# Keys with queries, and decays, loaded with 128 rows, and a new order of all queues planned for loads of 385 GB/s

## The chip, the cores and the metric

One core of a Trainium2 chip runs the kernel. Its engines work side by side, each through its own list of instructions in order: PE (TensorE, the matmuls; its weight loads are listed as PEld), DVE (VectorE), ACT (ScalarE), POOL (GpSimd), and SP (SyncE), which here only issues DMAs. An instruction that waits for another engine or for a DMA holds up everything behind it on its own engine. The metric is the device time of one execution in microseconds (us), lower being better. The kernel before took 775.98 us in the median of three runs (774.26 to 776.66).

## The reference

```python
for t in range(S):                                    # S = 768, per batch (4) and head (8), head_dim D = 48
    state = alpha[:, :, t, :, None] * state + np.einsum('bhd,bhe->bhde', k[:, :, t], v[:, :, t])
    y[:, :, t] = np.einsum('bhd,bhde->bhe', q[:, :, t], state)
x = y.transpose(0, 2, 1, 3).reshape(4 * 768, 384)     # 3072 tokens
h = x @ w_in;  x = (h * np.cos(h)) @ w_out            # first MLP, 384 -> 2048 -> 384
h = np.maximum(np.maximum(x @ w1, x @ w2), x @ w3)    # second MLP, 384 -> 768 -> 384
out = h @ w_out2
```

A linear attention with a decay per key dimension feeds two dense layers in a row. All inputs are float32.

## The kernel before, in words

The 3072 tokens are cut into six units of 512. In each unit attention goes by four pairs of heads; a pair's keys and queries, and its decays, lie with one head in partitions 0 to 47 and the other in 64 to 111, so that 112 rows are used. Per pair three loads come in on SP's queue: decays `al` (112 x 522 float32), keys with queries `kq` (112 x 1024) and values `v` (128 x 384). The recurrence is done in chunks. DVE forms running products of the decays by scans, POOL multiplies the keys by one of them and the queries by the other, PE transposes keys and multiplies, DVE masks the products with a triangle, PE multiplies the masked products by the values. Unit 0, where no state comes in, is done by `att0` with chunks of 128; units 1 to 5 are done by `turn` and `visit` with chunks of 64, slipped between the matmuls of the first MLP of the unit before.

The dense layers run in three passes of a rounded format: each float32 factor is split into a high part and a low part, and high x high, low x high and high x low are added. In the first MLP a step (`moe1`, 96 of them, 16 a unit) takes nine matmuls of 128x128 by 128x512 into one PSUM bank (lines L658 to L660), then cos on ACT and DVE (L666 to L684), then nine matmuls into three accumulators (L689 to L691). The second MLP (L740 to L765) takes unit after unit when all six have passed the first.

The weights of the first MLP, 32 blocks of 384 KB, two for each of 16 steps (`wi` and `wo`), come as raw 8-byte words into four buffers `raw`. Each block is converted when it has landed: ACT makes a top half (L360), DVE joins words (L361), ACT rounds to the high part (L365), and the low part is a subtraction. For the `wi` blocks that is POOL's (L369, into `wil`). For the `wo` blocks, `LOD = (1, 3)` makes it DVE's (L367, into `wol`), and the joined words then stand in a PSUM bank.

The order of all work is set in advance. `build` records every operation with its engine, an estimated duration, what it reads and writes, and a due time. `Program.order` then plays the program through with these estimates, each engine taking among its ready operations the one with the smallest due time, and the sequence it arrives at is written out as the program. The constants at the head of the file (`FIRST`, `ATT0`, `ATTS`, `W1E`, `EARLY`, `V2` and so on) set due times; `LANDED` and a rate for DMAs set when a load is taken to have landed. Where the plan has PE idle for long enough early on, it puts matmuls that nobody reads (L909).

Places to find in the code below: `att0` with the loads at L411 to L413, the scans at L418 and L424, POOL's products at L420 and L426, the masks at L458, values by masked products at L473, and the split of a result into high (ACT, L489) and low part. For pair `k < XLE` the low part is made by PE and ACT (L491, L492), else by DVE (L494). `prepare` with the loads at L509 to L511, the scans L514 and L518, and POOL's products L517 and L520; `visit` with its matmuls at L556, L560, L574 and L581.

Of the kernel before, what the change touches and what calls it, by code (L numbers as in the profile page):

```python
# [62 lines left out]

XLE = 1
MKP = 0
GATE, GSTEP = 1, 1
LOD = (1, 3)

W1E = 12
MOE_EARLY = 4  # L70
EARLY = 3
FIRST = -4
ATT0 = -1
ATTS = 3.3
VIS, VEND, VQ = 4.0, 13, 0.2
LARGE, STALL, PATIENT = 2, 0.6, 1.5
V2, V2S, TA = 16.0, 3.2, 1.0
NA = (NU - 1) * NP
# [5 lines left out]
class Program:  # L84
# [9 lines left out]
    def __init__(self):  # L94
        self.ops = []
        self.last_write = {}
        self.readers = {}
        self.of_bank = {}

    def op(self, eng, dur, fn, reads=(), writes=(), due=0.0, nbytes=None, port=False, tiled=False, count=6):  # L100
        n = len(self.ops)
        deps = set()
        for k in reads:
            if k in self.last_write:
                deps.add(self.last_write[k])
# [12 lines left out]
        deps.discard(n)
        port = port or (eng == "Pool" and nbytes is None)
        self.ops.append((eng, dur, nbytes, fn, sorted(deps), due, port, tiled, count))  # L120
        return n

    def order(self, banks, limit):
# [50 lines left out]
        for _ in range(n):  # L174
# [32 lines left out]
            if nbytes is not None:  # L207
                dma_free = max(dma_free, end + (0.65 if e == "SP" else 1.05)) + nbytes / 295e3
                end = dma_free + LANDED
# [65 lines left out]

HW, LANDED, SLACK = 0.46, 1.6, 0.0


@with_exitstack
def tile_kernel(ctx, tc, aa, qk, vv, wt, outT):  # L280
# [32 lines left out]

    kq_b = [ap.tile([PR, 2 * HB], F32, name=f"kq{i}") for i in range(NKQ)]
    v_b = [ap.tile([P, N2, 2, D], F32, name=f"v{i}") for i in range(NV)]
# [74 lines left out]
    def att0(k, p, t0):  # L390
        na, nk, nv, n2 = k % NIN, k % NKQ, k % NV, k % 2
        t, kq_, v, s = al_b[na], kq_b[nk], v_b[nv], s_b[p]
        vk, kk_ = ("v", nv), nk
        gf, kg = g_b[k % NGS], ("g", k % NGS)
        if k == 2:
            v, vk = q_b[2][:, 0:2 * N2 * D].rearrange("p (i j e) -> p i j e", i=N2, j=2), ("q", 2)
        if k == 3:
            v, vk = v_b[2], ("v", 2)
            t, na = inv_b[0], "iv0"
            gf, kg = inv_b[1][:, 0:AL], ("iv1",)  # L400
            kq_, kk_ = yy_b[1].bitcast(F32).rearrange("p a b -> p (a b)")[0:PR], "yy1"
        g = gf[:, 0:AP].rearrange("p (c t) -> p c t", c=N2)
# [97 lines left out]
    def prepare(n, t0):  # L500
# [271 lines left out]
    def build():  # L772
# [210 lines left out]
```

## Time and profile before

| | |
|---|---|
| runs of before, us | 774.26, 776.66, 775.98 |
| profiled execution, us | 773.87 |
| its span, us | 772.1 |
| PE busy | 762.5 us, 99% |
| DVE busy | 429.4 us, 56% |
| ACT busy | 348.4 us, 45% |
| POOL busy | 125.3 us, 16% |
| granted clock of TensorE | 1.0 throughout |

The span is from the first to the last instruction on the core; the profiled execution's own time is 1.8 us more. A share over the whole span says little here, since the first 90 us, with attention of two units and the weights' conversion, are full on every engine, and the rest is matmuls almost alone. PE's busy share counts matmuls that wait in the array for each other: a matmul of 512 columns is listed with some 390 ns, while in a dense stretch one starts every 0.23 us. So PE's loss is read from the starts of its instructions.

### The profile page before, as it was taken

How to read it: one execution, taken by the hardware profiler on the slowest of the kernel's cores; microseconds unless marked ns; L12 is line 12 of the kernel's file. 1: busy time of each engine (PE TensorE's matmuls, PEld its weight loads, DVE VectorE, ACT ScalarE, POOL GpSimd, SP SyncE). 2: the span in 40 equal slices, each digit the busy share in tenths (PEclk: the TensorE clock that was granted, in tenths of full speed). 3: DMA queues.
4: the chain of work that ended last, by engine and by line, in shares of the span. 5: the costliest groups of instructions: out<-in, count | busy, mean ns of one | idle time of the engine just before them, and what ended most of it. 6: DMA issues, size and time to landing. Idle time of an engine off the chain costs nothing.

```text
span 772.1 us, 14185 instructions
## 1 busy us (share of the span) xinstructions
PE 762.5 (99%) x5863; PEld 626.0 (81%) x5863; DVE 429.4 (56%) x720; ACT 348.4 (45%) x669; POOL 125.3 (16%) x133
## 2 busy tenths in 40 slices
PE   8899999999999999999999999999999999999998
PEld 6687788888888888888888888888888888888886
DVE  8799998686856776765557754432221312213121
ACT  5688756455555655465568754411121211111121
POOL 5555432120301121110023301100000000000000
PEclk9999999999999999999999999999999999999999
DMA  9977633232311231121027504220020200200001
GB/s 287 277 236 217 190 106 102 54 97 75 110 53 55 86 110 43 42 90 36 8 82 269 168 20 138 88 81 28 14 96 28 82 27 14 96 24 4 22 20 42
DMA packets 26464, 69.84 MB, mean 90 GB/s; under 512 B 3392, under 2 KB 6464, under 8 KB 26400
## 3 DMA queue, kind: packets, MB, share of 16 engines
q1 hardware_dynamic: 26400, 68.93, 28.3%
q8 instruction: 46, 0.75, 0.4%
q14 instruction: 18, 0.15, 0.1%
HBM read 52.80 MB, written 14.16 MB: 87 GB/s over the span
## 4 chain that ended last, share of the span: by engine, by line
PE 88%; DVE 1%; ACT 1%; issue 0%; DVEq 0%; ACTq 0%
PE ps L740 10%; PE ps L742 10%; PE ps L741 9%; PE acc L689 8%; PE acc L691 8%; PE ps L658 8%; PE acc L690 8%; PE ps L659 7%; PE ps L660 7%; PE ps L765 3%; PE ps L763 3%; PE ps L764 3%; PE ps L556 1%; PE ps L574 1%; PE ps L581 1%; PE ps L530 1%
## 5 line engine op out<-in xcount | busy, mean ns | idle before, releaser
L658 PE MATMUL ps<-xt,wih 128*128 128x512 f32 x288 | 115.1, 400 | 0.6 <-ACT woh L365 0.6
L689 PE MATMUL acc<-gh,woh 128*128 128x512 f32 x288 | 114.0, 396 | 0.1
L691 PE MATMUL acc<-gl,woh 128*128 128x512 f32 x288 | 112.4, 390 | 0.4 <-DVE gl L684 0.4
L659 PE MATMUL ps<-xt,wih 128*128 128x512 f32 x288 | 112.4, 390 | 0.2 <-DVE xt L494 0.2
L660 PE MATMUL ps<-xt,wil 128*128 128x512 f32 x288 | 112.3, 390 | 0.0
L690 PE MATMUL acc<-gh,wol 128*128 128x512 f32 x288 | 112.2, 390 | 0.0
L667 DVE SCALAR_TENSOR_TENSOR q<-q,ps 128x512 f32<-128x512 int32 x96 | 65.4, 682 | 49.8 <-ACT q L666 49.5
L750 DVE TENSOR_TENSOR ps<-t,ps 128x512 f32<-128x512 f32 x36 | 25.1, 696 | 106.7 <-PE ps L742 106.7
L666 ACT ACTIVATE q<-ps 128x512 int32<-128x512 f32 x96 | 57.1, 595 | 59.6 <-PE ps L660 58.0
L668 ACT ACTIVATE q<-q 128x512 f32<-128x512 f32 x96 | 60.5, 631 | 42.0 <-DVE q L667 41.3
L672 DVE TENSOR_TENSOR gl<-q,gh 128x512 fp32r<-128x512 f32 x80 | 57.8, 724 | 32.9 <-ACT gh L671 30.5
L751 ACT ACTIVATE h<-ps 128x512 fp32r<-128x512 f32 x36 | 21.6, 600 | 113.4 <-DVE ps L750 113.4
L670 DVE TENSOR_TENSOR q<-q,ps 128x512 f32<-128x512 f32 x80 | 54.7, 684 | 27.5 <-ACT q L668 26.5
L671 ACT ACTIVATE gh<-q 128x512 fp32r<-128x512 f32 x80 | 50.2, 629 | 35.1 <-DVE q L670 32.1
L748 DVE TENSOR_TENSOR t<-t,ps 128x512 f32<-128x512 f32 x36 | 24.8, 688 | 71.3 <-PE ps L742 71.2
L691 PEld LDWEIGHTS acc<-gl,woh 128*128 128x128 f32 x288 | 54.1, 188 | 12.7 <-DVE gl L684 1.3
L658 PEld LDWEIGHTS ps<-xt,wih 128*128 128x128 f32 x288 | 54.1, 188 | 12.5 <-ACT woh L365 1.0
L689 PEld LDWEIGHTS acc<-gh,woh 128*128 128x128 f32 x288 | 54.0, 188 | 12.2 <-ACT gh L679 0.5
L660 PEld LDWEIGHTS ps<-xt,wil 128*128 128x128 f32 x288 | 54.1, 188 | 11.7 <-POOL wil L369 0.5
L659 PEld LDWEIGHTS ps<-xt,wih 128*128 128x128 f32 x288 | 54.1, 188 | 11.4 <-DVE xt L494 0.9
L690 PEld LDWEIGHTS acc<-gh,wol 128*128 128x128 f32 x288 | 54.1, 188 | 10.5
L768 ACT ACTIVATE y<-ps 128x512 f32<-128x512 f32 x18 | 10.8, 600 | 93.2 <-PE ps L765 93.2
(147 smaller groups left out, 1449.1 us busy)
## 6 DMA issues: line engine op xcount, KB each, us to landing
raw<-in_wt SPq DMA_DIRECT2D x56, 384.0 KB, 3.8
kq<-in_qk SPq DMA_DIRECT2D x23, 448.0 KB, 4.3
x1d<-yy SPq DMA_DIRECT2D x18, 512.0 KB, 2.7
xt<-x1d SPq DMA_DIRECT2D x18, 512.0 KB, 5.0
al<-in_aa SPq DMA_DIRECT2D x23, 228.4 KB, 2.7
outT<-y SPq DMA_DIRECT2D x18, 256.0 KB, 2.0
v<-in_vv SPq DMA_DIRECT2D x23, 192.0 KB, 4.6
xt<-yy SPq DMA_DIRECT2D x30, 64.0 KB, 3.1
```

Source lines behind the costliest of these rows:

```text
L658: pe.matmul(ps, wi["h"][:, f, cc], xt[:, cc, 0], start=(cc == 0), stop=False)
L659: pe.matmul(ps, wi["h"][:, f, cc], xt[:, cc, 1], start=False, stop=False)
L660: pe.matmul(ps, wi["l"][:, f, cc], xt[:, cc, 0], start=False, stop=(cc == NR - 1))
L667: op("DVE", dve(HB), lambda: ve.scalar_tensor_tensor(q, q.bitcast(I32), -TWOPI, ps, ALU.mult, ALU.add), [hk], [qk], m)
L668: op("Act", act(HB), lambda: se.activation(q, q, AF.Sin, bias=0.5 * math.pi), (), [qk], m)
L672: op("DVE", dve(HB), lambda: ve.tensor_tensor(gl, q, gh.bitcast(F32), ALU.subtract), [qk, ("gh", gn)], [("gl", gn)], m, port=True)
L689: pe.matmul(acc[c], oh, gh, start=(f == 0), stop=False)
L690: pe.matmul(acc[c], ol, gh, start=False, stop=False)
L691: pe.matmul(acc[c], oh, gl, start=False, stop=(f == NF1 - 1))
L740: pe.matmul(ps, w2t["h"][m][:, f, cc], xt[:, cc, 0], start=(cc == 0), stop=False)
L741: pe.matmul(ps, w2t["h"][m][:, f, cc], xt[:, cc, 1], start=False, stop=False)
L742: pe.matmul(ps, w2t["l"][m][:, f, cc], xt[:, cc, 0], start=False, stop=(cc == NR - 1))
```

## The change

Five edits are made in one.

1. `kq` and `al` get 128 rows instead of 112, on the host as in SBUF; the loads move all 128. Views of the first 112 rows do the arithmetic as before, so no other instruction changes its shape.
2. `XLE` goes from 1 to 3: for pairs 1 and 2 of unit 0 also, the low part is made by one matmul and an ACT copy instead of a DVE subtraction.
3. `LOD = (1,)`: every second `wo` block now stays in SBUF, and its low part is POOL's (8 blocks of 32).
4. In `att0` the masked products go through three buffers in turn (two `a` and the second `q`) instead of two.
5. The planner takes 385 GB/s for loads instead of 295 and 1.0 us until landing instead of 1.6; its constants are other ones, and single events are shifted in their due times by a table. The new rule with `HOLD` is empty and never applies.

```diff
-XLE = 1
+XLE = 3
...
-LOD = (1, 3)
-
-W1E = 12
...
+LOD = (1,)
+
+W1E = 7
...
+HOLD, HOLD_END = {}, 32.0
...
+        if eng != "PE" or not self.fixed:
+            due += self.shift[nbytes is not None]
...
-                dma_free = max(dma_free, end + (0.65 if e == "SP" else 1.05)) + nbytes / 295e3
+                dma_free = max(dma_free, end + (0.65 if e == "SP" else 1.05)) + nbytes / RATE
...
-HW, LANDED, SLACK = 0.46, 1.6, 0.0
+RATE = 385e3
+HW, LANDED, SLACK = 0.46, 1.0, 0.0
...
-    kq_b = [ap.tile([PR, 2 * HB], F32, name=f"kq{i}") for i in range(NKQ)]
+    kq_f = [ap.tile([P, 2 * HB], F32, name=f"kq{i}") for i in range(NKQ)]
+    kq_b = [t[0:PR] for t in kq_f]
...
-        op("SP", HW, lambda: nc.sync.dma_start(kq_, qk[0, p]), (), [kk, kq], first - 3.9, dma(PR * 2 * HB * 4))
+        op("SP", HW, lambda: nc.sync.dma_start(kq_to, qk[0, p]), (), [kk, kq], first - 3.9, dma(P * 2 * HB * 4))
...
-        aks = [[("a", j, 0), ("a", j, 1)] for j in range(2)]
+        slots = [(a_b[j].rearrange("p a b c -> p (a b) c").rearrange("p a c -> p (a c)"), [("a", j, 0), ("a", j, 1)]) for j in range(2)] + [(q_b[1], [("q", 1)])]
+        slots = [slots[(2 * k + j) % 3] for j in range(2)]
...
-        for _, _, f, a in sorted(events):
+        for n, (_, _, f, a) in enumerate(sorted(events)):
+            G.shift, G.fixed = SHIFT.get(n, (0.0, 0.0)), f is moe1
             f(*a)
+        G.shift, G.fixed = (0.0, 0.0), True
...
-    aa = _np.ascontiguousarray(aa.reshape(NU, NP, 2 * UP, ALW)[:, :, :PR])
-    qk = _np.ascontiguousarray(qk.reshape(NU, NP, 2 * UP, 2 * HB)[:, :, :PR])
+    aa = aa.reshape(NU, NP, P, ALW)
+    qk = qk.reshape(NU, NP, P, 2 * HB)
```

Lines of the changed file lie 13 to 17 lower: its L372, L374, L380 and L382 are L359, L361, L367 and L369 of before; L475, L511, L526 to L528, L531, L533 and L537 are L458, L494, L509 to L511, L514, L516 and L520.

What it moves is seen at three places. The first is SP's queue after the first twelve loads, the first four weight blocks and the decays of the next pair (`raw_89` to `raw_92` are the four raw buffers, `al_`, `kq_` and `v_` a pair's loads). Before:

```order
L510 DMA kq_104<-in_qk 112x1024
L509 DMA al_125<-in_aa 112x522
L511 DMA v_107<-in_vv 128x384
L510 DMA kq_105<-in_qk 112x1024
L509 DMA al_126<-in_aa 112x522
L510 DMA kq_106<-in_qk 112x1024
L359 DMA raw_90<-in_wt 128x1536
L359 DMA raw_89<-in_wt 128x1536
L511 DMA v_108<-in_vv 128x384
L359 DMA raw_92<-in_wt 128x1536
L359 DMA raw_91<-in_wt 128x1536
```

And in the changed program, from the same place:

```order
L527 DMA kq_104<-in_qk 128x1024
L526 DMA al_125<-in_aa 128x522
L527 DMA kq_105<-in_qk 128x1024
L526 DMA al_126<-in_aa 128x522
L528 DMA v_107<-in_vv 128x384
L372 DMA raw_89<-in_wt 128x1536
L372 DMA raw_90<-in_wt 128x1536
L527 DMA kq_106<-in_qk 128x1024
L528 DMA v_108<-in_vv 128x384
L372 DMA raw_91<-in_wt 128x1536
L372 DMA raw_92<-in_wt 128x1536
```

The fifth and sixth weight block stand ahead of one load of keys now, and the seventh and eighth behind it.

The second place is DVE at the end of unit 0's attention: masks (into `a_` and `q`), scans (into `g_` and `al_`), joined words of the weights (`raw_`, `ps_`), low parts (`wol`, `xt_`). Before, from the low part of the second weight block to the mask pair of the last pair of heads and the scan behind it:

```order
L367 TENSOR_TENSOR wol<-ps_103,woh 128x384
L458 TENSOR_TENSOR a_110<-ps_100,tri_120 128x512
L458 TENSOR_TENSOR a_111<-ps_101,tri_120 128x512
L494 TENSOR_TENSOR xt_327<-acc_97,xt_327 128x512
L361 SCALAR_TENSOR_TENSOR raw_91<-raw_91,top_93 128x384
L361 SCALAR_TENSOR_TENSOR ps_100<-raw_92,top_94 128x384
L367 TENSOR_TENSOR wol<-ps_100,woh 128x384
L514 SCALAR_TENSOR_TENSOR g_127<-al_124,one_121 112x520
L494 TENSOR_TENSOR xt_327<-acc_96,xt_327 128x512
L516 RECIPROCAL inv_122<-g_127 112x8
L458 TENSOR_TENSOR a_110<-ps_99,tri_120 128x512
L458 TENSOR_TENSOR a_111<-ps_103,tri_120 128x512
```

In the changed program, from the low part of the same block:

```order
L380 TENSOR_TENSOR wol<-ps_103,woh 128x384
L374 SCALAR_TENSOR_TENSOR raw_91<-raw_91,top_93 128x384
L374 SCALAR_TENSOR_TENSOR raw_92<-raw_92,top_94 128x384
L475 TENSOR_TENSOR a_111<-ps_102,tri_120 128x512
L475 TENSOR_TENSOR q<-ps_99,tri_120 128x512
L531 SCALAR_TENSOR_TENSOR g_127<-al_124,one_121 112x520
L374 SCALAR_TENSOR_TENSOR raw_89<-raw_89,top_93 128x384
L533 RECIPROCAL inv_122<-g_127 112x8
L475 TENSOR_TENSOR a_110<-ps_100,tri_120 128x512
L475 TENSOR_TENSOR a_111<-ps_103,tri_120 128x512
```

Two low parts of `xt` and one of `wol` are gone from DVE here, and the words of the fifth weight block (the second `raw_89`) now stand ahead of the last two masks.

The third place is POOL around the products of the first visit (`kq_104` with `g_127`, then with `al_124`), low parts of the weights (`wil`, `wol`) and the state `d_112`. Before:

```order
L369 TENSOR_TENSOR wil<-raw_91,wih 128x384
L517 TENSOR_TENSOR kq_104<-kq_104,g_127 112x512
L635 TENSOR_TENSOR d_112<-s_118,g_127 112x192
L520 TENSOR_TENSOR kq_104<-kq_104,al_124 112x512
L642 COPY kq_104<-kq_104 48x256 x2
L369 TENSOR_TENSOR wil<-raw_89,wih 128x384
L369 TENSOR_TENSOR wil<-raw_91,wih 128x384
```

In the changed program:

```order
L382 TENSOR_TENSOR wil<-raw_91,wih 128x384
L382 TENSOR_TENSOR wol<-raw_92,woh 128x384
L534 TENSOR_TENSOR kq_104<-kq_104,g_127 112x512
L382 TENSOR_TENSOR wil<-raw_89,wih 128x384
L652 TENSOR_TENSOR d_112<-s_118,g_127 112x192
L382 TENSOR_TENSOR wil<-raw_91,wih 128x384
L537 TENSOR_TENSOR kq_104<-kq_104,al_124 112x512
L382 TENSOR_TENSOR wol<-raw_92,woh 128x384
```

Two low parts, of the fifth and of the seventh weight block, now stand between the visit's two products, where none stood before. On PE the change puts all of unit 0's attention ahead of the first matmul of the first MLP (before, 12 of these stood ahead of the last pair's values and 6 behind the first visit's first half; now 18 stand behind the values and ahead of the visit), takes out the matmuls of L909, and adds two of L508 (L491 of before).

## Rows read from the trace of the kernel before

**Rows 1.** The page, its head and part 1.

```profile
span 772.1 us, 14185 instructions
PE 762.5 (99%) x5863; PEld 626.0 (81%) x5863; DVE 429.4 (56%) x720; ACT 348.4 (45%) x669; POOL 125.3 (16%) x133
```

**Rows 2.** Busy time by stage: stretch, each engine's busy us, clock, DMA share, GB/s.

```profile
0.00:24.37 24.37, 20.78 (x182) 16.30 (x183) 20.34 (x44) 13.83 (x36) 14.27 (x23) 1.00 0.97 286
24.37:32.71 8.34, 7.27 (x103) 5.44 (x102) 6.84 (x13) 3.76 (x9) 3.90 (x7) 1.00 1.02 328
32.71:38.12 5.41, 4.81 (x18) 3.04 (x17) 4.49 (x10) 5.41 (x12) 3.09 (x3) 1.00 0.66 201
38.12:92.00 53.88, 53.38 (x591) 42.44 (x590) 50.74 (x94) 46.16 (x96) 27.10 (x29) 1.00 0.77 224
92.00:768.00 676.00, 676.00 (x4974) 558.76 (x4973) 346.97 (x563) 278.68 (x519) 76.97 (x74) 1.00 0.21 69
```

**Rows 3.** Timeline of PE, 24 to 38 us: start, us, line, [idle before <-releaser].

```profile
24.37 0.40 PE L658 MATMUL ps<-xt,wih 128*128 128x512 f32 x1
...
28.12 1.08 PE L473 MATMUL acc<-a,v 128*48 128x128 f32 x16
30.04 0.69 PE L556 MATMUL ps<-kq 48*64 48x64 f32 x32 [0.84 <-POOL kq L520]
...
31.03 0.50 PE L658 MATMUL ps<-xt,wih 128*128 128x512 f32 x1
...
32.71 1.02 PE L909 MATMUL ps<-ident 128*128 128x512 f32 x2
...
36.37 0.47 PE L658 MATMUL ps<-xt,wih 128*128 128x512 f32 x1 [0.58 <-ACT woh L365]
...
38.12 0.39 PE L689 MATMUL acc<-gh,woh 128*128 128x512 f32 x1
38.35 0.39 PE L690 MATMUL acc<-gh,wol 128*128 128x512 f32 x1
```

**Rows 4.** Timeline of PE at 86 us.

```profile
86.63 0.50 PE L691 MATMUL acc<-gl,woh 128*128 128x512 f32 x1 [0.43 <-DVE gl L684]
```

**Rows 5.** Timeline of DVE, first scan to the words of block five.

```profile
3.71 1.27 DVE L418 TENSOR_TENSOR_SCAN g<-al,acc 112x258 f32<-112x258 f32 x2 [0.56 <-DMA al<-in_aa]
...
24.04 0.56 DVE L367 TENSOR_TENSOR wol<-ps,woh 128x384 fp32r<-128x384 f32 x1 [0.69 <-ACT woh L365]
...
25.66 0.66 DVE L494 TENSOR_TENSOR xt<-acc,xt 128x512 fp32r<-128x512 f32 x1
26.24 0.19 DVE L516 RECIPROCAL inv<-g 112x8 f32<-112x8 f32 x1
26.35 1.24 DVE L458 TENSOR_TENSOR a<-ps,tri 128x512 f32<-128x512 f32 x2
27.51 1.23 DVE L518 TENSOR_TENSOR_SCAN al<-al,inv 112x520 f32<-112x520 f32 x1
30.24 0.57 DVE L361 SCALAR_TENSOR_TENSOR ps<-raw,top 128x384 uint32<-128x384 uint32 x1 [1.50 <-ACT top L360]
```

**Rows 6.** Timeline of ACT, the fifth weight block's landing.

```profile
29.57 0.63 ACT L360 ACTIVATE top<-raw 128x384 f16<-128x384 bf16 x1 [0.80 <-DMA raw<-in_wt]
```

**Rows 7.** Stretches as in rows 2: weights, pairs' loads, 512-KB loads.

```profile
14.90:17.80 2.90, 2.61 (x29) 2.21 (x28) 2.87 (x7) 2.42 (x6) 2.02 (x2) 1.00 1.04 402
19.80:22.80 3.00, 2.72 (x32) 2.07 (x28) 2.74 (x6) 1.81 (x5) 2.38 (x4) 1.00 1.05 292
512.50:516.50 4.00, 4.00 (x20) 3.30 (x18) 1.38 (x2) 0.68 (x2) 0.00 (x0) 1.00 0.95 366
```

**Rows 8.** Groups by form, 0 to 100 us: xcount | busy, mean ns | idle before.

```profile
L369 POOL TENSOR_TENSOR wil<-raw,wih 128x384 fp32r<-128x384 f32 x16 | 17.0, 1060 | 20.6 <-ACT wih L365 17.3 <-DMA xt<-yy 2.0 <-issue 1.1
L361 DVE SCALAR_TENSOR_TENSOR raw<-raw,top 128x384 uint32<-128x384 uint32 x16 | 9.7, 607 | 0.0
L367 DVE TENSOR_TENSOR wol<-ps,woh 128x384 fp32r<-128x384 f32 x16 | 8.8, 550 | 2.7 <-ACT woh L365 2.5
```

More of the change, by code (lines that the diff above doesn't have):

```diff
@@ L61 @@
 GLP1 = 4
-XLE = 1
+XLE = 3
 MKP = 0
 GATE, GSTEP = 1, 1
-LOD = (1, 3)
-W1E = 12
[L70 to L77, printed above, removed]
+LOD = (1,)
+W1E = 7
+MOE_EARLY = 3
+EARLY = 5
+FIRST = -6
+ATT0 = -2
+ATTS = 3
+VIS, VEND, VQ = 4.0, 13, 1.0
+HOLD, HOLD_END = {}, 32.0
+SHIFT = {5: (0.2, 0.0), 12: (0.8, 0.0), 26: (-1.8, 0.0), 29: (2.9, 0.0), 35: (0.0, 0.1), 59: (0.4, 0.0), 60: (2.4, 0.0), 66: (0.7, 0.0)}
+LARGE, STALL, PATIENT = 2, 0.3, 3
+V2, V2S, TA = 17, 2.8, 0.5
 NA = (NU - 1) * NP
@@ L98, in __init__ @@
         self.of_bank = {}
+        self.shift, self.fixed = (0.0, 0.0), True
     def op(self, eng, dur, fn, reads=(), writes=(), due=0.0, nbytes=None, port=False, tiled=False, count=6):
         n = len(self.ops)
+        if eng != "PE" or not self.fixed:
+            due += self.shift[nbytes is not None]
         deps = set()
@@ L184, in order @@
             i = min((e == "PE" and stall(j) > STALL, self.ops[j][5], j) for j in waiting[e] if ready(j) <= t)[2]
+            if e in HOLD and t < HOLD_END:
+                soon = [(r, j) for j in waiting[e] if self.ops[j][5] < self.ops[i][5] - 1.0 for r in (ready(j),) if t < r < t + HOLD[e] * self.ops[i][1]]
+                if soon:
+                    t, i = min(soon)
             waiting[e].remove(i)
@@ L325, in tile_kernel @@
     one0 = ap.tile([PR, AL], F32, name="one0").rearrange("p (c t) -> p c t", c=NC)
-    inv_b = [ap.tile([PR, KO], F32, name=f"inv{i}") for i in range(2)]
+    inv_f = [ap.tile([P, KO], F32, name=f"inv{i}") for i in range(2)]
+    inv_b = [t[0:PR] for t in inv_f]
     inv0 = [t[:, 0:AL].rearrange("p (c t) -> p c t", c=NC) for t in inv_b]
-    al_b = [ap.tile([PR, KO], F32, name=f"al{i}") for i in range(NIN)]
+    al_f = [ap.tile([P, KO], F32, name=f"al{i}") for i in range(NIN)]
+    al_b = [t[0:PR] for t in al_f]
     g_b = [ap.tile([PR, AL], F32, name=f"g{i}") for i in range(NGS)]
@@ L392, in att0 @@
         t, kq_, v, s = al_b[na], kq_b[nk], v_b[nv], s_b[p]
+        al_to, kq_to = al_f[na], kq_f[nk]
         vk, kk_ = ("v", nv), nk
@@ L399, in att0 @@
             t, na = inv_b[0], "iv0"
+            al_to = inv_f[0]
             gf, kg = inv_b[1][:, 0:AL], ("iv1",)
-            kq_, kk_ = yy_b[1].bitcast(F32).rearrange("p a b -> p (a b)")[0:PR], "yy1"
+            kq_to = yy_b[1].bitcast(F32).rearrange("p a b -> p (a b)")
+            kq_, kk_ = kq_to[0:PR], "yy1"
         g = gf[:, 0:AP].rearrange("p (c t) -> p c t", c=N2)
@@ L410, in att0 @@
         first = FIRST - 20 + k
-        op("SP", HW, lambda: nc.sync.dma_start(t, aa[0, p, :, 0:KO]), (), [kf], first - 4 - (0.8 if k else 0), dma(PR * KO * 4))
-        op("SP", HW, lambda: nc.sync.dma_start(kq_, qk[0, p]), (), [kk, kq], first - 3.9, dma(PR * 2 * HB * 4))
+        op("SP", HW, lambda: nc.sync.dma_start(al_to, aa[0, p, :, 0:KO]), (), [kf], first - 4 - (0.8 if k else 0), dma(P * KO * 4))
+        op("SP", HW, lambda: nc.sync.dma_start(kq_to, qk[0, p]), (), [kk, kq], first - 3.9, dma(P * 2 * HB * 4))
         op("SP", HW, lambda: nc.sync.dma_start(v, vv[0, p]), (), [vk], first - 3.7, dma(P * HB * 3))
@@ L448, in att0 @@
         op("PE", SLOW * 0.9, umm, [tk, vk], [uk], t0 - 0.8, count=16)
-        aj = [a_b[j].rearrange("p a b c -> p (a b) c").rearrange("p a c -> p (a c)").rearrange("p (i t) -> p i t", i=N2) for j in range(2)]
-        aks = [[("a", j, 0), ("a", j, 1)] for j in range(2)]
+        slots = [(a_b[j].rearrange("p a b c -> p (a b) c").rearrange("p a c -> p (a c)"), [("a", j, 0), ("a", j, 1)]) for j in range(2)] + [(q_b[1], [("q", 1)])]
+        slots = [slots[(2 * k + j) % 3] for j in range(2)]
+        aj, aks = [x.rearrange("p (i t) -> p i t", i=N2) for x, _ in slots], [x for _, x in slots]
         for j in range(2):
@@ L508, in prepare @@
         kf, kk, kq, vk, ik = ("inf", na), ("ink", nk), ("inq", nk), ("v", nv), ("iv", n2)
-        op("SP", HW, lambda: nc.sync.dma_start(t, aa[u, p, :, 0:KO]), (), [kf], t0 - 4.8 + (0.8 if not k else 0), dma(PR * KO * 4), tiled=True)
-        op("SP", HW, lambda: nc.sync.dma_start(kq_, qk[u, p]), (), [kk, kq], t0 - 3.9, dma(PR * 2 * HB * 4), tiled=True)
+        op("SP", HW, lambda: nc.sync.dma_start(al_f[na], aa[u, p, :, 0:KO]), (), [kf], t0 - 4.8 + (0.8 if not k else 0), dma(P * KO * 4), tiled=True)
+        op("SP", HW, lambda: nc.sync.dma_start(kq_f[nk], qk[u, p]), (), [kk, kq], t0 - 3.9, dma(P * 2 * HB * 4), tiled=True)
         op("SP", HW, lambda: nc.sync.dma_start(v, vv[u, p]), (), [vk], t0 - 3.7, dma(P * HB * 3), tiled=True)
```

## The prediction

> **What bounds the kernel now.** I read the page's head first: PE is busy 762.5 of 772.1 us [rows 1], so only PE's own losses can be won back. Busy shares hide where these lie, so next come stretches [rows 2]. From 92 to 768 us PE shows no idle time, and the change neither drops nor shortens a matmul there; whatever it does must come from the first 92 us. There the matmuls of the first MLP begin at 24.37 us [rows 3], and PE is idle 3.6 us before that, 1.1 up to 32.71, 0.6 up to 38.12 and 0.5 up to 92 [rows 2]. Busy is too kind a word for PE, since matmuls overlap, so the timeline is read by starts: in a dense run one of 512 columns starts each 0.23 us (38.12, 38.35) [rows 3]. Between 32.71 and 38.12 there are 15 useful ones, 3.45 us; the stretch takes 5.41, so it loses 2.0. Two causes stand there: the filler matmuls of L909, started where the plan expected a hole, and a wait of 0.58 for a converted weight at 36.37 [rows 3]. After 38.12 little is lost: the largest wait is 0.43 at 86.63, for a low part from DVE [rows 4], and with what the pipe loses around it and a similar smaller hitch I put that stretch at about 1.0.
>
> Why is the weight late? DVE's timeline has it idle 1.50 us up to 30.24, behind ACT [rows 5]; ACT starts that block at 29.57 after waiting for its DMA [rows 6]. So in the first 30 us the loads bound a stretch, while DVE is busy 20.3 of 24.4 us [rows 2]. The DMA share is at 1.0 in both of the first two stretches, yet the rate differs by what moves: 402 GB/s while weight blocks of 128 rows move, 292 while pairs' loads, mostly of 112 rows, do [rows 7]. Later, loads of 128 rows with 4 KB a row (as `kq` will be) move 366 GB/s at a share of 0.95 [rows 7], which is 385 when full.
>
> **Loads (edit 1, and SP's order).** A `kq` load grows from 459 to 524 KB and an `al` load from 234 to 267. Before, between the first decays (3.71 us, rows 5) and the fifth weight block (29.57, rows 6) lie 6 `al`, 7 `kq`, 5 `v` and 5 weight loads: 7.56 MB in 25.9 us, 292 GB/s. After, one `kq` fewer stands ahead of it: 6, 6, 5 and 5, with the larger sizes 7.70 MB. At 385 this lands at 3.71 + 20.0 = 23.7 us, at 402 at 22.9, at 292 at 30.1. I take 23.7, the rate of the row whose loads have the same form. Six microseconds earlier is much, and worth nothing by itself: something must have waited for it.
>
> **Unit 0's attention on DVE (edits 2 to 4).** From the first scan to the end of the last mask pair it takes 3.71 to 26.35 + 1.24 = 27.59 [rows 5]. In this piece the new order drops two low parts of `xt` (0.66 each, rows 5) and one `wol` (0.55, rows 8), and adds one joining of words (0.61, rows 8): -1.26, so 26.3 with the same idle time. By the other route, the fifth block is joined just before those masks: landing 23.7, ACT 0.63 [rows 6], joining 0.61, reciprocal 0.19, masks 1.24 [rows 5], in all 26.4. Both agree and I take 26.4. The early end is 25.0, if two waits for ACT of 0.69 as at 24.04 [rows 5] go as well; the third buffer of masked products helps only there, since a mask no longer waits for an older product. The late end is 32.8, with the loads at 292.
>
> PE then does the last values (begun 0.2 later, 1.08 long, rows 3), 18 matmuls of the MLP at 0.23 and the first half of the first visit (30.04 to 31.03, 0.99, rows 3): 26.6 + 1.1 + 4.1 + 1.0 = 32.8. The same work was done at 32.71 before, when 12 of those matmuls ran in the waits of attention. So this step is worth nothing, between 1.3 won and 6.4 lost. The two added matmuls of L508 lie in PE's waits for the masks; without that cover they cost 0.5.
>
> **Steps 2 to 4 of the MLP.** The weights of step 2 (the fifth block) are joined at 25.0, rounded by ACT in about 0.6, subtracted by POOL in 1.06 [rows 8]: ready at 26.7 against a need at 32.8. The seventh block has 0.39 + 0.52 + 0.20 + 0.39 = 1.5 MB behind the fifth, lands at 27.6 and is ready at about 30.6 against a need two microseconds further on than the fifth's. So the wait at 36.37 goes, and no filler stands in its place. What is late next is the chain of cos for step 0, to the first matmul of L689; before, it came 38.12 - 32.71 = 5.4 after the point above, now 21 matmuls (4.8) lie in between, and as step 0 ends three matmuls before step 1 there is just room. I take 1.7 of the 2.0 as won (0.3 to 2.0).
>
> **38 to 92 us.** DVE is busy 50.7 of 53.9 us there [rows 2]. The eight low parts of `wo` that go to POOL take 8 x 0.55 = 4.4 off DVE, some before this stretch; on POOL they cost 8 x 1.06 = 8.5. Against that, the second visits come at shorter distances. Of 1.0 us lost I count 0.4 as won (1.5 lost to 1.0 won).
>
> **Sum.** 0 + 1.7 + 0.4 = 2.1 off the profiled execution's 773.87 (the span of 772.1 and 1.8 around it) gives 771.8. That execution lies 2.1 below the runs' median, and the four executions known have a mean of 775.2; on the scale of the runs the forecast lies between 773.1 and 773.9, and I say 773.5.
>
> **Rivals.**
> *More is won:* both waits for ACT go, masks end at 25.0, and the later losses go in full: 1.3 + 2.0 + 1.0 = 4.3, 771.3. For it: DVE is the engine that is relieved, and it is the full one. Against: every part at its best.
> *The loss moves:* the matmuls that filled attention's waits now stand behind it, so PE waits earlier instead of later, and the 1.7 are paid there: 775.2 to 775.6. For it: 12 matmuls, 2.8 us, lose that use.
> *POOL's queue (slower):* a visit's second product stands behind two low parts now and behind none before, and PE stood 0.84 us for that product already [rows 3]. If each of the four visits of unit 1 waits for one or two, that is 4 x 1.06 to 8 x 1.06, at the middle 6.3: 779.8. It decides once the low parts before the product end later than DVE's scan before it. Against it: POOL is busy 27.1 of 53.9 us [rows 2], some 32 with five more of the eight. The Trainium skill (SBUF — State Buffer, "Who interferes with whom") adds that a DVE instruction with two SBUF inputs and a GpSimd one that reads SBUF hold each other up for a whole instruction; by that the eight could cost DVE up to 8.5 us in its joinings. The trace does not bear out such a price: the joinings into SBUF take 607 ns on average beside 16 low parts on POOL [rows 8].
> *The loads gain nothing from 128 rows (slower):* at 292 GB/s the fifth block lands at 30.1 with DVE's last masks behind it, 6.4 later: 779.9. It decides where the 2.1 are used up, at 25.8, a mean of 349 GB/s. Against it: 366 and 402 in rows 7.
> *A ceiling between:* a mean of 358 lands the block at 25.2, 1.5 later: 775.0. The Trainium skill (DMA: Bandwidth & Descriptors, "Specifications") gives about 358 GB/s as HBM's limit for a core; 402 in this trace is above it.
>
> **How the numbers follow.** A measurement here can tell about 0.3%, 2.3 us, so faster is below 773.65 and slower above 778.3. Forecast 0.50 (own range 772.0 to 775.0, so 0.27 faster and 0.23 the same); more is won 0.17, faster; the loss moves 0.10, the same; POOL's queue 0.14, of it 0.13 slower; loads gain nothing 0.06, slower; the ceiling 0.03, the same. Sums: 0.44 faster, 0.37 the same, 0.19 slower. The range takes in more is won and most of the way to the slower cases: 770.6 to 778.4.
>
> **What would show it.** Right: between 5 and 25 us the rate near 385; ACT's start on the fifth block near 23.7; the last masks ended near 26.4; the first matmul of the MLP later than 24.37, at about 27.7, and from there dense to 38 but for 0.3; no PE wait for a weight; joinings on DVE as long as before. Wrong: PE waiting for a visit's keys or queries from POOL, DVE waiting for ACT at a block that has not landed, or new waits after 38 us. If the first matmul comes well ahead of 27.7, the first step was sized too small.

## The result: 0.7% slower, and where it went

The changed kernel took 781.29 us in the median of five runs (776.76 to 783.64), against 775.98 (774.26 to 776.66): a ratio of 1.0069, interval 1.005 to 1.0087. The forecast was 773.5, and the range up to 778.4 does not hold it. Of the five runs one, the profiled execution, took 776.76 at a granted clock of 0.999; the other four took 780.85 to 783.64 at mean clocks of 0.990 to 0.997. So two questions stand: what the profiled execution lost at full clock (776.76 against 773.87 in the profiled execution of before), and what the others lost with the clock.

The head of the profile after, which answers to [rows 1]: the span is 3.0 longer, DVE is 5 us less busy, POOL 7 us more.

```profile
span 775.1 us, 14208 instructions
PE 764.2 (99%) x5863; PEld 626.0 (81%) x5863; DVE 424.3 (55%) x710; ACT 348.4 (45%) x671; POOL 132.6 (17%) x141
```

The stages of after, cut at the same pieces of work as [rows 2] (first matmul of the first MLP, the first visit's first half done, first matmul of L706): busy us of each engine, clock, DMA share, GB/s.

```profile
0.00:28.53 28.53, 23.60 (x203) 18.06 (x204) 23.77 (x48) 16.85 (x42) 18.31 (x27) 1.00 0.91 346
28.53:34.23 5.70, 5.60 (x84) 4.15 (x83) 5.16 (x7) 5.17 (x12) 2.90 (x3) 1.00 0.77 245
34.23:39.46 5.23, 5.19 (x29) 3.97 (x22) 4.54 (x9) 4.96 (x11) 3.79 (x6) 1.00 0.66 204
39.46:92.00 52.54, 51.26 (x583) 40.95 (x582) 42.09 (x79) 39.34 (x82) 29.03 (x29) 1.00 0.63 196
92.00:768.00 676.00, 675.34 (x4964) 556.51 (x4963) 348.76 (x569) 281.45 (x529) 78.56 (x78) 1.00 0.22 73
```

PE's timeline at those cuts answers to [rows 3], where the same four stood at 24.37, 30.04, 31.03 and 38.12 (L675 and L706 are L658 and L689 of before, L573 is L556):

```profile
28.53 0.50 PE L675 MATMUL ps<-xt,wih 128*128 128x512 f32 x1
...
33.25 0.69 PE L573 MATMUL ps<-kq 48*64 48x64 f32 x32
...
34.23 0.50 PE L675 MATMUL ps<-xt,wih 128*128 128x512 f32 x1
...
39.46 0.40 PE L706 MATMUL acc<-gh,woh 128*128 128x512 f32 x1
```

Up to 39.46 the changed kernel is even: 39 matmuls are done there where before 33 were at 38.12, and six take 1.4. From there PE stands 1.28 us up to 92, where it stood 0.50, and 0.66 behind 92, where it stood nowhere. Its timeline shows the largest wait, which answers to the 0.43 of [rows 4]:

```profile
74.99 0.50 PE L706 MATMUL acc<-gh,woh 128*128 128x512 f32 x1 [0.87 <-ACT gh L696]
```

Why is `gh` late? ACT's timeline ahead of it: in order, it stood 1.99 for a weight block that had not landed, with cos for the MLP (L685) and `gh` (L696) queued behind.

```profile
71.70 0.64 ACT L373 ACTIVATE top<-raw 128x384 f16<-128x384 bf16 x1 [1.99 <-DMA raw<-in_wt]
72.21 0.60 ACT L685 ACTIVATE q<-q 128x512 f32<-128x512 f32 x1
...
74.36 0.58 ACT L696 ACTIVATE gh<-ps 128x512 fp32r<-128x512 f32 x1
```

And SP's queue, which issues that block at 66.76 only, behind a load of values that itself took 1.74 to go out:

```profile
64.92 1.74 SPq L528 DMA_DIRECT2D v<-in_vv  x1
66.76 0.37 SPq L372 DMA_DIRECT2D raw<-in_wt  x1
67.19 1.22 SPq L632 DMA_DIRECT2D xt<-yy  x2
```

ACT waits like that for blocks 5.9 us between 40 and 110 us, six times; before it was 1.0 us, twice. Taken by starts, the hitches of PE at 74 us (1.4 with the two matmuls behind), 81 (0.5), 106 (0.9), 256 (0.2) and 350 us (0.6) come to 3.6, against some 0.7 at 86 us before: that is nearly all of the 3.0 of the span. The one at 350 us has another cause, a product of DVE's (0.34 of wait).

### The profile page after: what moved, and what is told of

Same layout as the page of the kernel before. It is cut to its first block, busy times and chain, and to the rows that moved or that the text cites. A ratio compares the mean times of both kernels' runs of the same rounds, so it can differ in the third digit from the quotient of the medians.

```text
span 775.1 us, 14208 instructions
## 1 busy us (share of the span) xinstructions
PE 764.2 (99%) x5863; PEld 626.0 (81%) x5863; DVE 424.3 (55%) x710; ACT 348.4 (45%) x671; POOL 132.6 (17%) x141
## 4 chain that ended last, share of the span: by engine, by line
PE 89%; DMA 5%; ACT 2%; DVE 1%; issue 1%; SPq 1%; POOL 0%; ACTq 0%; DVEq 0%; POOLq 0%
PE ps L758 9%; PE ps L757 9%; PE ps L759 9%; PE acc L706 8%; PE acc L708 8%; PE acc L707 8%; PE ps L675 8%; PE ps L676 7%; PE ps L677 7%; DMA raw<-in_wt 4%; PE ps L780 3%; PE ps L781 3%; PE ps L782 3%; PE ps L573 1%; PE ps L591 1%; PE ps L598 1%
## 5 line engine op out<-in xcount | busy, mean ns | idle before, releaser
L706 PE MATMUL acc<-gh,woh 128*128 128x512 f32 x288 | 114.1, 396 | 1.5 <-ACT gh L696 1.2
L675 PE MATMUL ps<-xt,wih 128*128 128x512 f32 x288 | 115.2, 400 | 0.0
L685 ACT ACTIVATE q<-q 128x512 f32<-128x512 f32 x96 | 60.4, 630 | 39.8 <-DVE q L684 39.2
L689 DVE TENSOR_TENSOR gl<-q,gh 128x512 fp32r<-128x512 f32 x80 | 58.0, 727 | 27.0 <-ACT gh L688 24.5
L683 ACT ACTIVATE q<-ps 128x512 int32<-128x512 f32 x96 | 56.6, 590 | 32.8 <-PE ps L677 32.5
L706 PEld LDWEIGHTS acc<-gh,woh 128*128 128x128 f32 x288 | 54.0, 188 | 14.3 <-ACT gh L696 2.0
L675 PEld LDWEIGHTS ps<-xt,wih 128*128 128x128 f32 x288 | 54.1, 188 | 12.2 <-DVE q L691 0.5
```

Source lines behind the costliest of these rows:

```text
L675: pe.matmul(ps, wi["h"][:, f, cc], xt[:, cc, 0], start=(cc == 0), stop=False)
L685: op("Act", act(HB), lambda: se.activation(q, q, AF.Sin, bias=0.5 * math.pi), (), [qk], m)
L689: op("DVE", dve(HB), lambda: ve.tensor_tensor(gl, q, gh.bitcast(F32), ALU.subtract), [qk, ("gh", gn)], [("gl", gn)], m, port=True)
L706: pe.matmul(acc[c], oh, gh, start=(f == 0), stop=False)
```

## The experiments

All ran beside the kernel before, on three chips: e0 to e3 beside 774.36 us, e4, e5 and e7 beside 774.5, and e6, e8 and e9 beside 774.76. The changed kernel itself ran again on the first of these alone, so a comparison between the groups is one between chips. Nothing of the computation is left out in any. A ratio is to the kernel before, with its 95% interval. "The clock fell" means a mean granted clock of 0.997 or less in a run; in the kernel before that was one run of 69.

**The changed kernel again** (e0_again).

> The changed kernel once more, to see in a second profile where TensorE's granted clock falls. The profiled execution of the changed kernel took 776.76 us at a clock of 0.999, four others 780.85 to 783.64 at 0.990 to 0.997. Clock theory: the executions at or above 780 have a stretch at half clock in unit 0's attention, where PE is busy 9.6 of 12 us between 8 and 20 (17.3 of 20 before); a profile of one shows a granted clock under 0.8 in some 4-us stretch before 32 us, and 4 to 7 us are lost there. Rival, jitter of loads: the clock stays at 1.00 in every stretch before 92 us and the difference is in waits of ACT for raw weight blocks. Median 780 to 782 by both.

781.3 us in the median (775.37 to 784.67, 12 runs), ratio 1.007 [1.0043, 1.0097]. From 8 to 20 us PE is busy 9.9 of 12 us in the first profile of after and 11.1 in before. Four runs at clock 0.999 or 1.0 took 775.37 to 776.95, eight at 0.987 to 0.993 took 778.87 to 784.67. So the clock theory holds. The profile is of the longest. Its stretches of 4 us:

```profile
8.00:12.00 4.00, 2.29 (x18) 1.92 (x17) 3.79 (x10) 1.20 (x3) 3.11 (x3) 0.90 1.04 407
12.00:16.00 4.00, 3.66 (x24) 2.92 (x23) 3.27 (x6) 0.89 (x3) 2.70 (x3) 0.50 1.03 400
...
24.00:28.00 4.00, 4.00 (x26) 3.48 (x25) 2.10 (x4) 2.61 (x6) 1.22 (x2) 0.50 0.60 208
28.00:32.00 4.00, 4.00 (x23) 2.45 (x23) 1.66 (x3) 1.17 (x3) 0.78 (x1) 0.54 0.51 157
```

The first of them in the first profile of after:

```profile
8.00:12.00 4.00, 2.92 (x32) 2.46 (x32) 3.83 (x9) 1.75 (x5) 3.75 (x4) 1.00 1.03 408
```

The clock is at 0.50 (1.2 of 2.4 GHz) from before 12 to nearly 32 us. The loss lies there: in PE's timeline the matmul that after has at 39.46 starts 7.3 later, and the span is 7.9 longer (783.0 against 775.1).

```profile
46.73 0.40 PE L706 MATMUL acc<-gh,woh 128*128 128x512 f32 x1
```

What PE did ahead of the fall, its timeline:

```profile
7.67 1.02 PE L461 MATMUL ps<-v,kt 128*112 128x96 f32 x8 [0.63 <-ACT kt L450]
9.77 0.60 PE L447 MATMUL ps<-ident,kq 112*128 112x112 f32 x4 [1.07 <-POOL kq L436]
11.01 1.70 PE L461 MATMUL ps<-v,q 128*112 128x96 f32 x8 [0.63 <-ACT q L450]
```

It waits 1.07 for POOL; POOL's timeline, in turn, has it wait for pair 1's keys:

```profile
8.54 1.18 POOL L436 TENSOR_TENSOR kq<-kq,g 112x512 f32<-112x512 f32 x1 [2.16 <-DMA kq<-in_qk]
```

In the first profile of after POOL began that product at 7.89, and PE's pause was 0.44:

```profile
9.13 0.60 PE L447 MATMUL ps<-ident,kq 112*128 112x112 f32 x4 [0.44 <-POOL kq L436]
```

The new order puts pair 1's key product on POOL, which needs a load, ahead of pair 0's query product, and pair 1's transposes on PE (L447) ahead of pair 0's masked products (L457). Before, PE ran those in that place (L441), and the transposes (L431) behind them without a pause:

```profile
8.93 1.16 PE L441 MATMUL ps<-kq 48*128 48x128 f32 x16
10.03 0.60 PE L431 MATMUL ps<-ident,kq 112*128 112x112 f32 x4
```

That gave theory A: the order makes pauses on PE at 8 to 11 us, and behind them the clock falls.

**The loads alone** (e1_loads): the kernel before with edit 1, the order of all queues untouched.

```diff
-    kq_b = [ap.tile([PR, 2 * HB], F32, name=f"kq{i}") for i in range(NKQ)]
+    kq_f = [ap.tile([P, 2 * HB], F32, name=f"kq{i}") for i in range(NKQ)]
+    kq_b = [t[0:PR] for t in kq_f]
...
```

> The kernel before with edit 1 alone: decays and keys with queries move 128 rows, the order of every queue as before. If the loads bound the stretch from 24 to 33 us, as the prediction reads it, the fifth weight block lands at about 24.5 instead of 29.5 and the 1.5 us of DVE's wait and the wait at 36.4 go: 1.0 to 2.5 us less than before, 773.5 to 775. If the loads move no faster with 128 rows: 0 to 2 us more. If loads were hidden anyway: the same within 0.7.

774.28 (773.19 to 777.2, 12 runs), ratio 0.9994 [0.9979, 1.0009]: nothing, so the loads alone did not bound the kernel before. In one run of the 12 the clock fell (0.996, the longest, 777.2). Its first stage, to be set beside that of [rows 2]:

```profile
0.00:24.37 24.37, 21.06 (x182) 16.80 (x183) 20.37 (x44) 13.85 (x36) 14.32 (x23) 1.00 0.94 355
```

And PE's timeline, beside [rows 3] (lines lie 3 to 6 lower than before's):

```profile
30.02 0.69 PE L562 MATMUL ps<-kq 48*64 48x64 f32 x32 [0.85 <-POOL kq L526]
...
35.97 0.47 PE L664 MATMUL ps<-xt,wih 128*128 128x512 f32 x1 [0.38 <-ACT woh L368]
...
37.73 0.40 PE L695 MATMUL acc<-gh,woh 128*128 128x512 f32 x1
```

The rate rises from 286 to 355 GB/s, and PE has the same waits at the same places; the one for a weight shrinks from 0.58 to 0.38. The matmul that stood at 38.12 comes at 37.73, and that 0.4 is gone again behind 92 us, where PE now stands 0.41. Why did the earlier landing win so little? ACT, in order, has the state `z` ahead of the fifth block and waits 3.05 for POOL there; it starts the block at 28.77, without a wait for the load, where it stood at 29.57 [rows 6]. So of the block's lateness only 0.8 was the load's.

```profile
27.54 0.36 ACT L651 ACTIVATE z<-d 48x192 f32<-48x192 f32 x1 [3.05 <-POOL d L641]
```

**112 rows again** (e2_rows112): the changed kernel with its order, loads as before.

```diff
-        op("SP", HW, lambda: nc.sync.dma_start(kq_to, qk[0, p]), (), [kk, kq], first - 3.9, dma(P * 2 * HB * 4))
+        op("SP", HW, lambda: nc.sync.dma_start(kq_, qk[0, p]), (), [kk, kq], first - 3.9, dma(P * 2 * HB * 4))
...
```

> The changed kernel with 112 rows moved as before, all queues in the changed order. If faster loads are what the changed order needs, the fifth block lands near 29 behind two masks of unit 0 and PE's first matmul of the MLP comes 4 to 6 us later than 28.5: 785 to 788. If the loss of the change lies in the order itself and loads matter little, 780 to 783.

783.17 (782.5 to 787.46, 6 runs), ratio 1.0119 [1.0092, 1.0147]; the clock fell in all six. That lies between the two forecasts, and their signs are mixed: the first matmul of the MLP came at 32.76, 4.2 later than in after, but the fall of the clock is in that too. In the mean it is 4 us above e0_again (784.4 against 780.4). The new order loses more without the faster loads, and loses with them too. In its profile the clock kept 1.00 through pauses of 0.64, 0.87 and 0.63 up to 11 us, and fell behind a longer one at 18 us:

```profile
20.18 0.79 PE L508 MATMUL acc<-yy,gl 128*128 128x512 f32 x1 [2.02 <-ACT yy L506]
```

The stretch behind it:

```profile
20.00:24.00 4.00, 3.82 (x23) 3.50 (x25) 3.19 (x6) 3.44 (x9) 2.70 (x5) 0.50 1.04 264
```

**Seven small products in four of PE's waits** (e3_fill), none of them in the pause at 8.7 us.

```diff
...
+                pe.matmul(ps_b[m][:, 0:P], ident, ident, start=True, stop=True)
```

> The changed kernel with seven small matmuls that nobody reads (128x128 by 128x128 of the identity) in four of PE's waits in unit 0's attention (between 7 and 18 us). Clock theory: PE's busy share from 8 to 20 us rises to that of before, the clock stays at 1.00 and the executions come down to that of the profiled one, 776 to 777.5. Rival, jitter of loads or waits after 60 us: no difference, 780 to 783. If the fillers stand in the way of attention, 0.3 to 1 us more than without.

778.13 (776.43 to 782.82, 12 runs), ratio 1.0047 [1.003, 1.0065]; the clock fell in 3 runs of 12, and the median is 0.6 above the theory's range: fewer falls, but not none. Its profile, one of the three, has a pause of 1.35 ahead of pair 1's transposes, at 9.81, and a clock of 0.50 from 12 to 16 us behind it; that pause was the one without a filler.

**Four of them in the pause itself** (e5_pause).

```diff
+    spare = {192: (chosen[("ps", "s0", 15)], 4)}
...
```

> Changed kernel, its order untouched, with four small 128x128 products of the identity (about 0.31 us each by the run with fillers) put on PE behind pair 0's first products (L461), in the pause before pair 1's transposes. They write a PSUM tile that nobody reads. Theory A (the pause brings the clock down): clock 0.998 or above in nearly all runs and a median of 775.5 to 777.5; pair 1's transposes begin at most 0.8 us later. Rival B (the clock falls because PE is lightly loaded for the whole of 8 to 24 us): the clock still falls in about half of the runs, and the median is 778 to 781. Rival D (it falls because of the transposes' late start alone, by some other way than the pause): as without them, 781.

778.15 (777.06 to 779.16, 8 runs), ratio 1.0038 [1.0024, 1.0053]. The clock was 0.999 or 1.0 in all eight, as A has it and neither B nor D. The two later kernels with the same fillers, e6_queue and e8_land, kept it too: 31 runs of 31, against 5 of 17 of the changed kernel. The time is 0.7 above A's range. In the profile the first MLP starts 0.4 later than in after, but only 0.1 of that is left when its 40th matmul starts (39.55), so where the rest goes is open. The fillers both end the pause and give PE work in it; the runs do not tell these two apart. In the profile they stand in the pause (four products, listed as eight matmuls):

```profile
8.97 1.08 PE L930 MATMUL ps<-ident 128*128 128x128 f32 x8
9.89 0.55 PE L447 MATMUL ps<-ident,kq 112*128 112x112 f32 x4
```

and the stretch has its full clock:

```profile
8.00:12.00 4.00, 3.26 (x28) 2.98 (x28) 3.79 (x9) 1.25 (x4) 3.35 (x3) 1.00 1.04 408
```

**Pair 0 in its old place, with masks and values** (e4_pair0). The numbers are the planner's; each triple takes an instruction out and sets it ahead of (0) or behind (1) another.

```diff
+    for i, j, d in [(158, 186, 0), (157, 185, 0), (161, 192, 0), (163, 221, 0), (164, 221, 0), (167, 226, 0)]:
+        order.remove(i)
+        order.insert(order.index(j) + d, i)
```

> Changed kernel; in unit 0's attention pair 0 goes as in the kernel before: POOL makes pair 0's query product ahead of pair 1's key product, PE runs pair 0's 16 masked products (L457) ahead of pair 1's transposes, DVE's masks and PE's value products of pair 0 follow at once. Nothing is left out. Theory A (TensorE's clock): in the changed kernel PE stands still 0.44 to 1.35 us before pair 1's transposes because POOL waits for pair 1's keys, and the granted clock then goes to 0.5 for 7 to 20 us in most executions, which costs 3 to 6 us. Then here PE has work in that stretch, the clock stays at 0.998 or above in nearly all runs, and the median falls from 781.3 to 775.5 to 777. Rival B (the clock falls because of something else in the first 12 us, such as the loads): 779 to 782 as before, with clocks of 0.987 to 0.996 in more than half of the runs. Rival C (the order after 40 us is the main cost, the clock only noise between chips): 777 to 779 whatever the clock.

779.99 (778.85 to 780.34, 6 runs), ratio 1.0062 [1.0045, 1.0078]: a miss, and a telling one. PE is dense at 8 to 12 us as hoped (3.37 of 4 us busy), but with the value products gone from their later place a pause opens at 17 us instead, and the clock falls behind that one (0.995 to 0.997 in all six runs). PE's timeline:

```profile
18.42 0.49 PE L508 MATMUL acc<-yy,gl 128*128 128x512 f32 x1 [1.36 <-ACT yy L506]
```

The stretches around it:

```profile
16.00:20.00 4.00, 2.64 (x23) 2.06 (x20) 3.93 (x10) 3.95 (x9) 3.75 (x5) 0.91 1.04 406
20.00:24.00 4.00, 4.00 (x26) 2.95 (x27) 1.56 (x3) 1.92 (x5) 2.51 (x3) 0.50 1.01 366
```

**Three instructions moved** (e9_query_first): pair 0's query product, scan and masked products back ahead of pair 1, the rest as changed.

```diff
+    for i, j, d in [(158, 186, 0), (157, 185, 0), (161, 192, 0)]:
+        order.remove(i)
+        order.insert(order.index(j) + d, i)
```

> Changed kernel with three instructions moved and nothing else: POOL makes pair 0's query product ahead of pair 1's key product, DVE ends pair 0's scan ahead of pair 1's second scan, and PE runs pair 0's 16 masked products (L457) ahead of pair 1's transposes. Unlike the run where the masks and value products of pair 0 were moved too, no wait of 1.36 us for ACT at L508 should come at 17 to 18 us, since the value products stay where the changed kernel has them. Nothing is left out and no filler is added. Theory A (the order in the first 10 us makes PE's pause, and the clock falls behind it): clock 0.998 or above in nearly all runs, median 775.5 to 777. Rival B (the clock falls from something else of the changed kernel): clocks of 0.987 to 0.996 in more than half of the runs, median 779 to 782.

778.07 (776.3 to 778.62, 5 runs), ratio 1.0035 [1.0022, 1.0048]; the clock stayed in four runs of five, without any filler, though on a chip where the changed kernel itself did not run. The pause is gone, as PE's timeline shows, for the masked products fill it; the time again lies 1 above A's.

```profile
9.38 1.16 PE L457 MATMUL ps<-kq 48*128 48x128 f32 x16
10.52 0.60 PE L447 MATMUL ps<-ident,kq 112*128 112x112 f32 x4
```

**The reverse** (e7_before_pause): the kernel of e1_loads with pairs 0 and 1 in the changed order.

```diff
+    for i, j, d in [(195, 177, 0), (196, 178, 0), (181, 205, 1), (183, 181, 1), (184, 183, 1), (263, 184, 1)]:
+        order.remove(i)
+        order.insert(order.index(j) + d, i)
```

> The reverse test: the kernel before with loads of 128 rows (774.3 us when it ran alone) and with pair 0 and 1 of unit 0's attention in the changed kernel's order: POOL makes pair 1's key product ahead of pair 0's query product, PE runs pair 1's transposes and products ahead of pair 0's masked products. All else is in the order of before, and nothing is left out. Theory A: a pause of 0.4 to 1.4 us on PE at about 9 us, and the clock at 0.5 for some 7 to 20 us behind it in more than half of the runs: 777 to 780 in those, 774.5 to 776 in the others. Rival B (the clock falls because of something else of the new order): clock 0.999 in nearly all runs and 774 to 776. Rival C: 774 to 776 whatever the clock.

779.52 (775.44 to 780.73, 10 runs), ratio 1.0052 [1.0033, 1.0071]. The clock fell in 8 runs of 10 (778.4 to 780.73); the two others took 775.44 and 775.49. Moving a scan, a product and 16 small matmuls in the first 12 us takes the kernel before from 774.3 to 779.5. With e5_pause, on the same chip, the effect is shown in both directions: the order brings the clock down, and work in its pause holds it. PE's timeline:

```profile
9.94 0.60 PE L437 MATMUL ps<-ident,kq 112*128 112x112 f32 x4 [0.37 <-POOL kq L426]
```

Its stretches:

```profile
8.00:12.00 4.00, 2.46 (x16) 2.08 (x17) 3.29 (x7) 1.69 (x4) 2.74 (x3) 0.88 1.04 409
12.00:16.00 4.00, 3.15 (x23) 2.69 (x22) 0.91 (x2) 0.65 (x2) 1.89 (x2) 0.50 1.03 400
```

**SP's queue at 65 us** (e6_queue): e5_pause, with the late weight block ahead of the load of values, and the copies `xt<-yy` behind two more blocks.

```diff
+    for i, j, d in [(118, 589, 0), (328, 128, 1), (329, 328, 1)]:
+        order.remove(i)
+        order.insert(order.index(j) + d, i)
```

> The changed kernel with the four small products in the pause (778.15 at full clock in all runs) and two moves in SP's queue near 65 us: the weight block that ACT waited 1.67 us for at 71.45 is issued ahead of the load of values that stood before it, and the two copies xt<-yy (L632), which wait for a low part from DVE, are issued behind the next two weight blocks instead of ahead of them. Theory (the loads stand behind waiting DMAs in SP's queue, and ACT, in order, holds cos for the MLP behind a block that has not landed): ACT's wait at 71.45 falls below 0.5, PE's wait of 0.62 between 72 and 76 us goes, and the median falls by 0.5 to 1.2 to about 777.3. Rival (the wait belongs to DVE's and ACT's own load there): ACT starts the block earlier but PE still waits 0.4 or more before L706 at 73 to 74 us, median unchanged.

776.95 (774.8 to 779.17, 12 runs), ratio 1.0025 [1.0014, 1.0036]. The block is issued at 65.24 (66.52 in e5_pause), ACT waits 0.16 for it where it waited 1.67, and `gh` is made 1.3 earlier than in e5_pause. ACT's timeline:

```profile
69.84 0.65 ACT L373 ACTIVATE top<-raw 128x384 f16<-128x384 bf16 x1 [0.16 <-DMA raw<-in_wt]
...
72.66 0.58 ACT L696 ACTIVATE gh<-ps 128x512 fp32r<-128x512 f32 x1
```

PE, at the place where after waited 0.87, runs through:

```profile
73.69 0.39 PE L677 MATMUL ps<-xt,wil 128*128 128x512 f32 x1
73.92 0.39 PE L706 MATMUL acc<-gh,woh 128*128 128x512 f32 x1
```

The wait is shown to come from the order of SP's queue; which of the two moves counts is not shown, as they were made together. That it is worth 1.2 in the median is not shown, as the two ratios' intervals overlap and the chips differ; the span of the profile fell by 1.7.

**A landing of 1.6 us in the plan** (e8_land), on e5_pause.

```diff
-HW, LANDED, SLACK = 0.46, 1.0, 0.0
+HW, LANDED, SLACK = 0.46, 1.6, 0.0
...
```

> The changed kernel with the four small products in the pause, and with LANDED back at 1.6 us while the rate stays at 385 GB/s: the same program plans the order of all queues with loads taken to land 0.6 us later; up to about 32 us the order comes out as in the changed kernel, from there SP, ACT and POOL are ordered anew. Nothing is left out. Theory (the plan's landing of 1.0 leaves no slack, so weight blocks come later than their turn on ACT, and that costs 1 to 2 us of PE after 60 us): ACT's waits for weight blocks between 40 and 110 us fall from 5.9 us to below 3, PE's waits behind them go, median 776 to 777.5. Rival (the constants were searched together, and any one changed alone gives another order that is as good or worse): 778 to 780, with waits at other places.

776.76 (775.61 to 777.69, 11 runs), ratio 1.0022 [1.0013, 1.0031]. From some 36 us on the new plan orders not only SP, ACT and POOL anew but DVE and PE too, so the run is less clean than it was meant to be. Waits between 40 and 110 us (total, times, longest), ACT's for weight blocks:

```profile
ACT top L373 <- DMA raw<-in_wt: 2.4, 6, 1.1
```

PE's, where the theory wanted none:

```profile
PE ps L675 <- DVE s L653: 1.7, 1, 1.7
PE acc L706 <- ACT gh L696: 0.8, 1, 0.8
```

Part of the theory holds: ACT's waits for blocks fall from 5.3 us (e5_pause) to 2.4, and the time to the middle of its range. Part of the rival holds too: PE's wait for `gh` is still there (0.8, at 72 us), and a new one, of 1.7 for a state from DVE, stands at 92 us. A slack of 0.6 us alone is not the cure.

No kernel here beats the one before; the best are level with it or 0.2% behind.

## Why the prediction was wrong, step by step

*Loads:* the rate was right. Between 4 and 24 us that of after is 377 to 408 GB/s, and the fifth block landed at 24.5 (ACT's start), where 23.7 was forecast and 29.57 stood before [rows 6]. The rivals on the rate are out. But the reading of before, that in the first 30 us the loads bound a stretch, holds for 0.8 us at most: e1_loads, with the faster loads alone, wins nothing in the end.

*Unit 0's attention on DVE, and PE behind it:* this is the step that failed. It was put at nothing, and it failed in two ways.

Its size, at full clock: the last masks ended at 27.09 against 26.4, the MLP began at 28.53 against 27.7, and the piece of work forecast for 32.8 was done at 34.23, so 1.5 were lost and not 0. The masks' 0.7 is the block's landing, which ACT and DVE both wait for. ACT's timeline:

```profile
24.51 0.64 ACT L373 ACTIVATE top<-raw 128x384 f16<-128x384 bf16 x1 [1.87 <-DMA raw<-in_wt]
```

And DVE's:

```profile
25.24 0.59 DVE L374 SCALAR_TENSOR_TENSOR raw<-raw,top 128x384 uint32<-128x384 uint32 x1 [1.15 <-ACT top L373]
...
25.86 1.23 DVE L475 TENSOR_TENSOR a<-ps,tri 128x512 f32<-128x512 f32 x2
```

Then the last values began 0.43 behind the masks, where the sum has 0.2; [rows 3] and [rows 5] had 0.53 (28.12 behind 27.59). The 18 matmuls took 4.7 (28.53 to 33.25), where the sum has 4.1: among other hitches a weight load waits for a low part that DVE still makes, at 31.15, behind the masks. The timeline of the weight loads:

```profile
31.89 0.19 PEld L676 LDWEIGHTS ps<-xt,wih 128*128 128x128 f32 x1 [0.52 <-DVE xt L511]
```

And its premise: it followed DVE and the loads and took PE's matmuls of that stretch to cost what they cost before, at a clock of 1.0 throughout. It never looked at what PE does while it waits there. The new order leaves PE's work in the first 12 us in pieces with pauses between, and the clock fell in 12 of the 17 runs of the changed kernel. In e0_again the eight of these took 782.4 in the mean, and the four others 776.3. In means that is 4.1 of the 5.7 us by which e0_again lies above the kernel before (780.4 against 774.7), and no term and no rival had it. The 1.6 left at full clock go with the new waits behind 60 us. With the clock held, e5_pause and e9_query_first still lie 3.3 and 2.9 above the kernel before, on other chips; why not 1.6 is open.

The Trainium skill (TensorE: Matmul & The Clock Gate, "HAM oscillation — how this bites in real kernels") tells of a kernel whose PE falls back to the low clock each time it waits for a load. The traces agree on the two levels (1.00 and 0.50) and on a wait for a load ahead of the fall (POOL's 2.16 for pair 1's keys in e0_again, behind which PE stood 1.07).

*Steps 2 to 4 of the MLP:* right. From 34.23 to 39.46 lie 21 matmuls, 4.8, in 5.2 us: 0.4 lost where 2.0 were, so 1.6 won against 1.7 forecast. No filler and no wait for a weight stand there. It paid for the lateness of the step before it, and nothing was left over: up to here it went as in the rival *the loss moves*.

*38 to 92 us:* 0.4 won was forecast, within 1.5 lost; about 1.2 was lost by PE's starts, 0.8 by its idle time. The term rested on DVE's relief, which came (42.1 of 52.5 us busy, 50.7 of 53.9 before [rows 2]). What became late was ACT, through loads that the plan takes to land 1.0 us after their transfer and that SP's queue held up. "New waits after 38 us" stood among the signs of being wrong, and no price was worked out for them.

*92 us and on:* put at nothing, since whatever the change does must come from the first 92 us. That was wrong: PE has hitches at 106, 256 and 350 us now, 1.7 in all. At full clock the steps come to 1.5 - 1.6 + 1.2 + 1.7 = 2.8 lost, of the 2.9 between the two profiled executions.

*POOL's queue*, the slower rival, did not come: from 24 us on no matmul of PE waits for a visit's product from POOL, and two of the weight loads wait 0.6 in all. Nor did the joinings on DVE get longer (597 ns on average over 24, 607 before [rows 8]). That rival had the right side, slower, by a mechanism that is not there.

## What to carry to other kernels

Where an order is made anew, go through PE's starts in the lightly filled stretches and list its pauses with what ends each; a piece that waits for a load should not stand ahead of one that is ready, since pauses of 0.4 to 1.1 us in the first 12 us cost some six through the clock here. Time such a kernel many times and read the granted clock of each run, as one profile can show either case. And where engines work in order, a load that lands early wins little while the engine has something else to wait for ahead of it (ACT in e1_loads), and a load that is issued late holds up what is ready behind it (ACT at 71 us in after).

## What the runs showed of the hardware

The clock fell although no single pause was long: behind 0.63, 1.07 and 0.63 us in e0_again, behind 0.63, 0.37 and 0.63 in e7_before_pause, while the first profile of after kept its clock through 0.63, 0.44 and 0.64, and that of e2_rows112 through 0.64, 0.87 and 0.63. What tells these apart is open; the pauses' sum does not. Once down, the clock stayed at 0.50 from 12 to 28 us in e0_again, with PE busy 3.6 to 4.0 of each 4 us.

Between 8 and 24 us all loads together, weights included, moved 400 to 408 GB/s in after, where those of pairs have 128 rows, and 264 to 360 in e2_rows112, in the same order with 112 rows.
